# One-core attention and two weight stages on Trainium2: when the first weights are decoded, and which engine adds up the value means

## The chip, the cores and the metric

The kernel runs on one core of one Trainium2 chip. A core has TensorE (matmuls, PE in the profile; its weight loads are PEld), VectorE (DVE), ScalarE (ACT), GpSimd (POOL), and SyncE (SP), which issues the DMAs. The engines run side by side, each works through its own queue in order, and they wait for each other with semaphores. The metric is the device time of one execution in microseconds (us). Three runs of the kernel before gave 589.56, 590.07 and 591.69 us; the median is 590.07.

## The reference

The inputs are q, k, v of shape (2, 8, 768, 64) and seven weight matrices in 64-bit floats. What is computed, cut to the core:

```
k_sum = k.reshape(B, H, 24, 32, D).max(axis=3)        # block maxima of the keys
v_sum = v.reshape(B, H, 24, 32, D).mean(axis=3)       # block means of the values
scores = concat([scale*q@k.T where |i-j| < 16 else -1e9, scale*q@k_sum.T + log(32)])
x = softmax(scores) @ concat([v, v_sum])              # -> 1536 tokens x 512
h = max(x @ w1, x @ w2, x @ w3) @ w_out               # 512 -> 768 -> 512
y = ((h @ w_a) * (h @ w_b)) @ w_out2                  # 512 -> 1536 -> 512
```

## The kernel before

Each of the two sequences (batch entries) is cut into two chunks of 384 tokens, and each chunk's attention into four groups, one per pair of heads. So the first sequence has groups 0 to 7: groups 0 to 3 are the first chunk, 4 to 7 the second. `steps(b)` traces the attention of a sequence in small steps; one group passes through `scores` (TensorE products, a masked minimum on VectorE in L190, the exponential on ScalarE in L191), `normal` (a reciprocal on VectorE in L199, the scaling on GpSimd in L201), `transposes` (TensorE L211, copies to `aT` by VectorE L213 and ScalarE L215) and `values` (TensorE L228, then the split of x into a high and a low part by ScalarE L368 and VectorE L369). The groups overlap by one stage. Keys, value windows and mean inputs are loaded only at a sequence's first chunk.

`means` gives the block means of the values: the transposed values arrive in the tile `full` by one DMA (L138), blocks are halved by GpSimd additions as often as `VSUM` says (L143: none for groups 0 and 1, five halvings for group 2, one for group 3), VectorE reduces the rest (L145), GpSimd copies the sums to a second place (L146), TensorE transposes them (L148), and ScalarE writes them, scaled by 1/32, among the value rows (L150).

A weight tile (128x512 64-bit numbers, tile `w`) takes three steps. `w_load` is the DMA (L286). `w_round` makes 32-bit numbers out of the halves: ScalarE L300 or VectorE L298 for the high half, ScalarE L302 for the low one, VectorE L304 and L305, and GpSimd L306 for the sum. `w_split` makes two parts that TensorE multiplies fast: ScalarE L310, and the remainder by GpSimd, or for every third weight by VectorE (L311). `weights(n)` traces n weights further, with the loads four ahead.

The first layer (`layers12`) has 18 units per chunk of tokens, then the second layer's four outputs. One unit uses one weight tile: 12 TensorE products of 128x384 (`ph`, L365), evacuated by ScalarE (L390) or by a maximum on VectorE (L392); every third unit ends in a split (L368, and L369 on GpSimd). Units of the first chunk run alone for six turns (`TURNS`), then in turn with those of the second chunk, so that a weight is then used twice.

What sets the order: the instructions are traced in program order with waits worked out by the language, and a scheduler then decides each engine's order before the kernel runs; only SP keeps the traced order. `tc.issue_after(ins)` forbids the scheduler to put what is traced in its block ahead of `ins` on the engine of `ins`. In the kernel before, `weights(1)` is traced at the attention's steps 12, 16, ..., 40 of the first sequence (`PRE`), with no such bound; the dense layers and later weights are traced after these 44 steps, the weights behind the last reciprocal (L566 and L571).

Of the kernel before, what the change touches and what calls it, by code (L numbers as in the profile page):

```python
# [9 lines left out]
F32 = mybir.dt.float32  # L10
# [5 lines left out]
ALU = mybir.AluOpType  # L16
AX = mybir.AxisListType

B, H, S, D = 2, 8, 768, 64
P = 128  # L20
DM, FF1, FF2 = 512, 768, 1536
NTOK = B * S
BLOCK, WINDOW = 32, 16
NB = S // BLOCK
NT = S // P
NP = H // 2
HALF = 64
WIN = HALF + 2 * WINDOW
NC = WIN + NB
SEG = P + NB  # L30
# [8 lines left out]
Z_AT, KEY0 = (2 * WINDOW, WIN), (P - 2 * WINDOW, P + NB + 2 * WINDOW)  # L39
# [15 lines left out]
W64, W32, WBUFS, QB, SM, GB, BANKS = (6, 3), (4, 3), (24, 10), 3, 2, (12, 9), (2, 2, 1, 2, 2)  # L55


AHEAD, PRE, TURNS = (4, 1), (9, 4), (6, (24, 42), (42, 60))

EARLY, BIAS_DVE, SPLIT_DVE = 16, ((0, 1, 0), (0, 1, 0), (0, 0, 0)), ((0, 0, 1), (0, 0, 1), (1, 1, 1))
AT_DVE, VSUM = ((1, 0), (1, 1)), (0, 0, 5, 1, 0)


C_ID, C_ALL = 4 * NC, 4 * NC + P

MASK = {(t, a): (2 * a + (t == (NT - 1 if a else 0))) * NC for t in range(NT) for a in range(2)}

# [2 lines left out]
def attention_then_maxout_then_bilinear(ctx: ExitStack, tc: tile.TileContext, qt, kt, vt, vwin, wall, const, out):  # L72
    nc = tc.nc
# [3 lines left out]
    V, A, G, T = nc.vector, nc.scalar, nc.gpsimd, nc.tensor  # L77

    one = ctx.enter_context(tc.tile_pool(name="one", bufs=1))
# [13 lines left out]
    ps_c = ctx.enter_context(tc.tile_pool(name="ps_c", bufs=BANKS[4], space=PSUM))  # L93
    ps_m = ctx.enter_context(tc.tile_pool(name="ps_m", bufs=BANKS[3], space=PSUM))

    kept = one.tile([P, C_ALL + 2 * NC + NP * (NT + 1) * SEG], F32, name="kept")
    cols = iter(range(kept.shape[-1]))

    def take(n):

        at = [next(cols) for _ in range(n)][0]
        return kept[:, at:at + n]

    cst = take(C_ALL)
    ident = cst[:, C_ID:C_ID + P]
# [6 lines left out]

    v_t = [one.tile([NC, MAXT, 2, 2, D], F32, name=f"v{p}") for p in range(NP)]
    vpad = [take(NC) for _ in range(2)]


    groups = [(c, p) for c in range(NCH) for p in range(NP)]
# [5 lines left out]
    x_t, exps, a_t, last = {}, {}, {}, [None]  # L123

    def keys(b, p):

        kk = k_t[p].rearrange("p (t k) -> p t k", k=SEG)
        nc.sync.dma_start(out=kk[:, :, 0:P], in_=kt[b, p].rearrange("r (t k) -> r t k", k=P))

        k2 = sm_p.tile([P, NT + 1, 4, 2], F32, tag="k2", name="k2")  # L130
        V.tensor_reduce(k2, kk[:, :, 0:P].rearrange("p t (n k) -> p t n k", k=WINDOW), AX.X, ALU.max)
        k2 = k2.rearrange("p t n o -> p (t n o)")[:, 7:7 + 2 * NB].rearrange("p (o n z) -> p o n z", o=1, z=2)
        V.tensor_reduce(kk[:, :, P:SEG], k2.to_broadcast([P, NT + 1, NB, 2]), AX.X, ALU.max)  # L133

    def means(b, p):

        full = w64_p.tile([P, S], F32, tag="full", name="full", bufs=2)
        nc.sync.dma_start(out=full, in_=vt[b, p])  # L138
        full = full.rearrange("p (n k) -> p n k", k=BLOCK)
        k = BLOCK  # L140
        for _ in range(VSUM[p if b == 0 else NP]):
            k //= 2
            G.tensor_tensor(full[:, :, 0:k], full[:, :, 0:k], full[:, :, k:2 * k], ALU.add)  # L143
        z0, z1 = (vpad[p % 2][:, o:o + NB] for o in Z_AT)
        V.tensor_reduce(z0, full[:, :, 0:k], AX.X, ALU.add)  # L145
        G.tensor_copy(z1, z0)  # L146
        ps = ps_t.tile([NC, P], F32, tag="t", name="psvs")
        T.transpose(ps, vpad[p % 2], ident)  # L148
        for a, o in enumerate(Z_AT):
            A.activation(v_t[p][o:o + NB, :, a].rearrange("k i h d -> k i (h d)"),  # L150
                         ps[o:o + NB].rearrange("k (o e) -> k o e", o=1).to_broadcast([NB, MAXT, P]),
                         AF.Copy, scale=1.0 / BLOCK)

    def load(g):

        c, p = groups[g]
        b, t, n = CHUNKS[c]
        if t == 0:
            keys(b, p)
        nc.sync.dma_start(out=q_t[g % QB][:, 0:n], in_=qt[b, p].rearrange("r (t a m) -> r t a m", t=NT, a=2)[:, t:t + n])  # L160
        if g == 0:
            nc.sync.dma_start(out=cst, in_=const)

    def load_values(g):
        c, p = groups[g]
        b, t, n = CHUNKS[c]
        vw = vwin[b, p].rearrange("r (i a h d) -> r i a h d", a=2, h=2, d=D)[:, t:t + n]
        for a, z in enumerate(Z_AT):
            for r0, r1, to in ((0, z, 0), (z, WIN, z + NB)):
                if r0 < r1:  # L170
                    nc.sync.dma_start(out=v_t[p][to:to + r1 - r0, 0:n, a], in_=vw[r0:r1, :, a])
        if t == 0:
            means(b, p)

    def scores(g, i):

        c, p = groups[g]
        t, q = CHUNKS[c][1] + i, q_t[g % QB]
        if i == 0:
            exps[g] = (sm_p.tile([P, MAXT, 2, NC], F32, tag="s", name="s"),  # L180
                       sm_p.tile([P, MAXT, 2], F32, tag="sm", name="sm"))
        s, sm = (x[:, i] for x in exps[g])
        ps = ps_s.tile([P, 2, NC], F32, tag="s", name="ps")
        nm = sm_p.tile([P, 2], F32, tag="nm", name="nm", bufs=4)
        for a in range(2):
            k0 = t * SEG + KEY0[a]
            T.matmul(ps[:, a], q[:, i, a], k_t[p][:, k0:k0 + NC], start=True, stop=True)  # L187
            mask = cst[:, MASK[t, a]:MASK[t, a] + NC]

            V.tensor_tensor_reduce(s[:, a], ps[:, a], mask, -1.0 / D ** 0.5, 3e38, ALU.add, ALU.min, nm[:, a:a + 1])  # L190
            A.activation(s[:, a], s[:, a], AF.Exp, bias=nm[:, a:a + 1], scale=-1.0, accum_out=sm[:, a:a + 1])  # L191

    def normal(g):

        n = CHUNKS[groups[g][0]][2]
        s, sm = (x[:, 0:n] for x in exps[g])
        r = sm_p.tile([P, MAXT, 2, 1], F32, tag="r", name="r")[:, 0:n]
        A.activation(r, sm.rearrange("p i (a o) -> p i a o", o=1), AF.Copy, bias=1e-9)
        last[0] = V.reciprocal(r, r).ins  # L199
        s, r = s.rearrange("p i a k -> p (i a) k"), r.rearrange("p i a o -> p (i a) o")  # L200
        G.tensor_tensor(s, s, r.to_broadcast([P, 2 * n, NC]), ALU.mult)  # L201

    def transposes(g):
        at, n = exps.pop(g)[0], CHUNKS[groups[g][0]][2]
        a_t[g] = aT = sm_p.tile([NC, MAXT, 2, P], F32, tag="aT", name="aT")
        for i0 in range(0, n, 2):
            i1 = min(n, i0 + 2)
            ps = ps_t.tile([NC, 2, 2, P], F32, tag="t", name="pst")
            for i in range(i0, i1):
                for a in range(2):  # L210
                    T.transpose(ps[:, i - i0, a], at[:, i, a], ident)  # L211
            if AT_DVE[g >= len(groups) // 2][i0 // 2 % 2]:
                V.tensor_copy(aT[:, i0:i1], ps[:, 0:i1 - i0])  # L213
            else:
                A.activation(aT[:, i0:i1], ps[:, 0:i1 - i0], AF.Copy)  # L215
# [17 lines left out]
    def steps(b):  # L233


        first, end = (c * NP * len(SIZES) for c in (b, b + 1))
        load(first)
        if b == 0:
            load(first + 1)
        load_values(first)  # L240
        yield
        for g in range(first - 1, end):
            if g >= first:
                transposes(g)
                if b == 0 and g + 2 < first + NP:
                    load(g + 2)
                if (b or g + 1 >= first + NP) and g + 1 < end:
                    load(g + 1)
                if g + 1 < end:
                    load_values(g + 1)  # L250
                yield
            for i in range(MAXT):
                if g + 1 < end and i < CHUNKS[groups[g + 1][0]][2]:
                    scores(g + 1, i)
                    if i == CHUNKS[groups[g + 1][0]][2] - 1:
                        normal(g + 1)
                yield
            if g >= first:
                values(g)
                yield  # L260
# [74 lines left out]
    def weights(most):  # L335

        nonlocal w_done, w_room
        for _ in range(most):
            if w_done == len(seq) or w_room + room[w_done] > w_freed + WBUFS[w_done >= N12] or w_done == N12 and not gate:
                return  # L340
            w_room += room[w_done]
            w_done += 1
            ahead = min(AHEAD[0], W64[w_done + AHEAD[0] > N12] - 2)
            for n, (step, more) in enumerate(((w_load, ahead), (w_round, AHEAD[1]), (w_split, 0))):
                while w_at[n] < min(w_done + more, len(seq) if gate else N12):
                    step(w_at[n])
                    w_at[n] += 1
# [208 lines left out]
            q += 2  # L556


    for i in range(2):
        V.memset(vpad[i], 0.0)  # L560
    for n, _ in enumerate(steps(0)):
        weights(1 if n >= PRE[0] and n % PRE[1] == 0 else 0)


    turns = TURNS[0] * "0" + (N1 - TURNS[0]) * "01" + TURNS[0] * "1" + "00001111" + (N1 + 4) * "2" + (N1 + 4) * "3"
    behind = last[0]  # L566
# [73 lines left out]
```

## Time and profile before

| what | value |
|---|---|
| median of 3 runs | 590.07 us (589.56 to 591.69) |
| profiled execution | 591.21 us |
| its span in the trace | 589.3 us |
| PE busy | 551.3 us (94%) |
| DVE busy | 377.8 us (64%) |
| ACT busy | 278.7 us (47%) |
| POOL busy | 208.2 us (35%) |
| share of TensorE in the chain that ended last | 63% |

Busy time of TensorE is a union of pipelined matmuls, so 94% says that it seldom stood empty, not that it ran at its peak. The shares are averages over the whole span: the first 60 us, where attention starts up, and the 500 us after them look very different, so the stretches have to be read one by one.

### The profile page before, as it was taken

The page shows a single profiled execution, that of the slowest core. Times are in us where ns is not written, and L with a number is a line of the kernel's source. Part 1 is how long each engine was busy: PE and PEld are TensorE (multiplying, and loading weights), DVE is VectorE, ACT ScalarE, POOL GpSimd, SP SyncE. Part 2 cuts the span into 40 slices and gives each one's busy share as a digit, 9 for nine tenths or more (in the row PEclk, how much of TensorE's full clock was granted, in tenths as well). Part 3 has the DMA queues.
Part 4 walks back from the last instruction along what each step waited for, and adds up shares of the span by engine and source line. Part 5 has one row for each costly group of instructions (what it writes and reads, how often), then busy time and mean ns, then how long its engine had stood idle before and what let it go on. Part 6 is the DMA issues. An engine that isn't in the chain of part 4 may idle for free.

```text
span 589.3 us, 8831 instructions
## 1 busy us (share of the span) xinstructions
PE 551.3 (94%) x3272; PEld 513.3 (87%) x3272; DVE 377.8 (64%) x780; ACT 278.7 (47%) x667; POOL 208.2 (35%) x184
## 2 busy tenths in 40 slices
PE   4778999999999999998889899999999999999997
PEld 3567989999999999997888789999999989999985
DVE  4786398857213331249998775777696796883374
ACT  3777657444434332246675565653543544331220
POOL 0497269943001221035652433332341351330030
PEclk9959999999999999999999999999999999999999
DMA  9998035933211000052121123122212212000005
GB/s 265 344 273 247 36 110 190 298 73 107 63 47 48 1 1 1 1 222 85 52 72 43 66 72 108 37 72 72 71 41 77 98 37 72 2 1 0 1 17 198
DMA packets 31291, 53.32 MB, mean 90 GB/s; under 512 B 2448, under 2 KB 18832, under 8 KB 31248
## 3 DMA queue, kind: packets, MB, share of 16 engines
q1 hardware_dynamic: 31248, 52.75, 28.2%
q8 instruction: 26, 0.43, 0.3%
q14 instruction: 17, 0.14, 0.1%
HBM read 49.59 MB, written 3.15 MB: 89 GB/s over the span
## 4 chain that ended last, share of the span: by engine, by line
PE 63%; DVE 14%; DMA 7%; issue 5%; POOL 5%; ACT 5%; SPq 1%; POOLq 0%; ACTq 0%; DVEq 0%
PE ph L365 15%; PE qb L365 13%; PE py L365 7%; PE qg L365 5%; PE po L529 5%; DMA w<-wall 5%; PE po L527 5%; PE po L528 5%; POOL w L306 3%; DVE wt L311 3%; PE qd L365 3%; PE ps L187 2%; PE psv L228 2%; DVE hg L369 2%; DVE w L305 2%
## 5 line engine op out<-in xcount | busy, mean ns | idle before, releaser
L365 PE MATMUL ph<-x,wt 128*128 128x384 f32 x864 | 164.2, 343 | 3.8 <-DVE nm L190 2.0
L365 PEld LDWEIGHTS ph<-x,wt 128*128 128x128 f32 x864 | 150.7, 191 | 5.3 <-ACT wt L310 2.2
L306 POOL TENSOR_TENSOR w<-w,w 128x512 int32<-128x512 int32 x60 | 86.7, 1450 | 122.6 <-DVE w L305 73.5
L365 PE MATMUL qb<-yt,wt 128*128 128x384 f32 x576 | 114.2, 339 | 7.3 <-DVE t L496 2.0
L365 PEld LDWEIGHTS qb<-yt,wt 128*128 128x128 f32 x576 | 101.6, 188 | 14.0 <-DVE t L496 3.2
L368 ACT ACTIVATE hg<-t 128x384 fp32r<-128x384 f32 x72 | 36.9, 521 | 81.0 <-DVE t L392 36.0
L499 POOL TENSOR_TENSOR t<-t,ca 128x384 f32<-128x384 f32 x36 | 42.8, 1204 | 88.4 <-DVE t L498 85.7
L365 PE MATMUL qg<-yt,wt 128*128 128x384 f32 x288 | 59.4, 339 | 1.4 <-DVE t L498 0.6
L539 DVE TENSOR_TENSOR acc<-po,acc 128x512 f32<-128x512 f32 x60 | 40.8, 687 | 26.9 <-PE po L529 26.7
L527 PE MATMUL po<-wt,hg 128*128 128x512 f32 x144 | 56.4, 392 | 0.5 <-ACT hg L368 0.5
L528 PE MATMUL po<-wt,hg 128*128 128x512 f32 x144 | 56.5, 393 | 0.0
L529 PE MATMUL po<-wt,hg 128*128 128x512 f32 x144 | 55.8, 395 | 0.2 <-DVE hg L369 0.2
L365 PE MATMUL py<-hg,wt 128*128 128x384 f32 x288 | 55.1, 341 | 0.3 <-ACT hg L368 0.3
L365 PEld LDWEIGHTS qg<-yt,wt 128*128 128x128 f32 x288 | 50.9, 189 | 4.1 <-DVE t L498 0.9
L191 ACT ACTIVATE s<-s,nm 128x120 f32<-128x120 f32 x96 | 37.1, 388 | 33.3 <-DVE nm L190 32.9
L365 PEld LDWEIGHTS py<-hg,wt 128*128 128x128 f32 x288 | 49.6, 188 | 0.8 <-ACT hg L368 0.6
L392 DVE TENSOR_TENSOR t<-ph,t 128x384 f32<-128x384 f32 x48 | 26.3, 552 | 36.0 <-PE ph L365 31.6
L369 POOL TENSOR_TENSOR hg<-t,hg 128x384 fp32r<-128x384 f32 x24 | 26.8, 1116 | 61.8 <-ACT hg L368 61.8
L187 PE MATMUL ps<-kept,q 128*128 128x120 f32 x192 | 38.3, 319 | 10.6 <-DVE kept L133 7.7
L311 DVE TENSOR_TENSOR wt<-w,wt 128x512 fp32r<-128x512 f32 (+1 forms) x44 | 35.2, 799 | 20.0 <-ACT wt L310 20.0
L190 DVE CUSTOM_DVE_ANT_0 s<-ps,kept 128x120 f32<-128x120 f32 x96 | 24.6, 278 | 36.0 <-PE ps L187 35.4
L310 ACT ACTIVATE wt<-w 128x512 fp32r<-128x512 f32 (+1 forms) x60 | 35.0, 583 | 25.0 <-POOL w L306 12.6
(72 smaller groups left out, 789.1 us busy)
## 6 DMA issues: line engine op xcount, KB each, us to landing
w<-wall SPq DMA_DIRECT2D x60, 512.0 KB, 3.4
q<-qt SPq DMA_DIRECT2D x16, 384.0 KB, 7.2
kept<-kt SPq DMA_DIRECT2D x8, 448.0 KB, 6.9
full<-vt SPq DMA_DIRECT2D x8, 384.0 KB, 6.2
out<-acc SPq DMA_DIRECT2D x12, 256.0 KB, 2.0
v<-vwin SPq DMA_DIRECT2D x16, 144.0 KB, 5.4
v<-vwin SPq DMA_DIRECT2D x16, 96.0 KB, 5.7
v<-vwin SPq DMA_DIRECT2D x16, 48.0 KB, 6.7
```

What stands on the lines that cost most here:

```text
L187: T.matmul(ps[:, a], q[:, i, a], k_t[p][:, k0:k0 + NC], start=True, stop=True)
L191: A.activation(s[:, a], s[:, a], AF.Exp, bias=nm[:, a:a + 1], scale=-1.0, accum_out=sm[:, a:a + 1])
L306: G.tensor_tensor(w.bitcast(I32), w.bitcast(I32), lw.bitcast(I32), ALU.add)
L311: eng.tensor_tensor(w[:, 1], r, w[:, 0], ALU.subtract)
L365: T.matmul(ps, w[:, i, o:o + P], x[:, j], start=first and n == 0, stop=last and n == 2, skip_group_check=more)
L368: A.activation(dst[:, 0], src, AF.Copy)
L369: eng.tensor_tensor(dst[:, 1], src, dst[:, 0], ALU.subtract)
L499: G.tensor_tensor(t, t, cs[c, f], ALU.mult)
L527: T.matmul(ps, g[:, 0], w[:, 0], start=(f == 0), stop=False)
L528: T.matmul(ps, g[:, 0], w[:, 1], start=False, stop=False)
L529: T.matmul(ps, g[:, 1], w[:, 0], start=False, stop=(f == 1))
L539: V.tensor_tensor(acc[c, i], ps, acc[c, i], ALU.add)
```

## The change

Four things are edited.

- `PRE` is (18, 5): `weights(1)` is traced at steps 18, 23, 28, 33, 38 and 43 of the first sequence's attention, six times instead of eight. Step 17 holds the last reciprocal of the first chunk.
- Each of these calls stands in `tc.issue_after(behind)`, where `behind` is the last reciprocal traced in the step before.
- For the first sequence, `full` is loaded in another layout (tokens on partitions) from `vwin`, in two DMAs of 64 rows, and TensorE adds up the blocks: six products with a slice of a 0/1 matrix `ones` take the place of the VectorE reduction, the GpSimd additions and copy, and the transposition. `VSUM` is gone.
- `ones` is made once, of the identity matrix, by a memset, a reduction and a copy on VectorE. The second sequence's means are as they were with no GpSimd halving, which is what `VSUM[4] = 0` said before.

```diff
-AHEAD, PRE, TURNS = (4, 1), (9, 4), (6, (24, 42), (42, 60))
+AHEAD, PRE, TURNS = (4, 1), (18, 5), (6, (24, 42), (42, 60))
-AT_DVE, VSUM = ((1, 0), (1, 1)), (0, 0, 5, 1, 0)
+AT_DVE = ((1, 0), (1, 1))
...
         full = w64_p.tile([P, S], F32, tag="full", name="full", bufs=2)
-        nc.sync.dma_start(out=full, in_=vt[b, p])
-        full = full.rearrange("p (n k) -> p n k", k=BLOCK)
-        k = BLOCK
-        for _ in range(VSUM[p if b == 0 else NP]):
-            k //= 2
-            G.tensor_tensor(full[:, :, 0:k], full[:, :, 0:k], full[:, :, k:2 * k], ALU.add)
-        z0, z1 = (vpad[p % 2][:, o:o + NB] for o in Z_AT)
-        V.tensor_reduce(z0, full[:, :, 0:k], AX.X, ALU.add)
-        G.tensor_copy(z1, z0)
+        if b == 0:
+
+            vw = vwin[b, p, WINDOW:WINDOW + HALF].rearrange("r (i a e) -> r i a e", a=2, e=P)
+            for a in range(2):
+                nc.sync.dma_start(out=full[a * HALF:(a + 1) * HALF].rearrange("r (i e) -> r i e", e=P), in_=vw[:, :, a])
+        else:
+            nc.sync.dma_start(out=full, in_=vt[b, p])
         ps = ps_t.tile([NC, P], F32, tag="t", name="psvs")
-        T.transpose(ps, vpad[p % 2], ident)
+        if b == 0:
+
+            for t in range(NT):
+                at = NB - NS - t * NS
+                T.matmul(ps, ones[:, at:at + NC], full[:, t * P:(t + 1) * P], start=t == 0, stop=t == NT - 1)
+        else:
+            z0, z1 = (vpad[p % 2][:, o:o + NB] for o in Z_AT)
+            V.tensor_reduce(z0, full.rearrange("p (n k) -> p n k", k=BLOCK), AX.X, ALU.add)
+            G.tensor_copy(z1, z0)
+            T.transpose(ps, vpad[p % 2], ident)
...
             load(first + 1)
+            z0, z1 = (ones[:, NB - NS + z:NB + z] for z in Z_AT)
+            V.tensor_reduce(z0, ident.rearrange("p (j k) -> p j k", k=BLOCK), AX.X, ALU.add)
+            V.tensor_copy(z1, z0)
...
     for n, _ in enumerate(steps(0)):
-        weights(1 if n >= PRE[0] and n % PRE[1] == 0 else 0)
+        if n >= PRE[0] and (n - PRE[0]) % PRE[1] == 0:
+
+            with tc.issue_after(behind):
+                weights(1)
+        else:
+            behind = last[0]
```

On VectorE, the stretch from the key maxima of group 3 to the reciprocals of groups 2 and 3 stands so before (L190 is a score's masked minimum, L298, L304, L305 and L311 are weights, L369 is the split of x):

```order
L133 TENSOR_REDUCE kept<-k_252 128x7x24
L213 COPY aT<-pst 120x512
L369 TENSOR_TENSOR x<-psv,x 128x384
...
L304 TENSOR_SCALAR w_315<-psw 128x512
L145 TENSOR_REDUCE kept<-full 128x24
L305 SCALAR_TENSOR_TENSOR w_315<-psw,w_315 128x512
L298 TENSOR_SCALAR psw<-w_304 128x512
...
L199 RECIPROCAL r<-r 128x6
L305 SCALAR_TENSOR_TENSOR w_516<-psw,w_516 128x512
L145 TENSOR_REDUCE kept<-full 128x24
L311 TENSOR_TENSOR wt<-w_390,wt 128x512
L304 TENSOR_SCALAR w_574<-psw 128x512
L199 RECIPROCAL r<-r 128x6
```

and so in the changed kernel (its L199 is the minimum, L208 the reciprocal, L222 the copy to aT, L381 the split of x, L316, L310 and L317 weights):

```order
L135 TENSOR_REDUCE kept<-k_263 128x7x24
...
L208 RECIPROCAL r<-r 128x6
L381 TENSOR_TENSOR x<-psv,x 128x384
L199 ISA s,nm<-ps,kept 128x120
...
L222 COPY aT<-pst 120x512
L208 RECIPROCAL r<-r 128x6
L316 TENSOR_SCALAR w_411<-psw 128x512
L310 TENSOR_SCALAR psw<-w_400 128x512
L317 SCALAR_TENSOR_TENSOR w_411<-psw,w_411 128x512
```

No weight instruction stands ahead of the fourth reciprocal any more; before, fourteen did.

On TensorE, the end of the first sequence's attention stands so before (psv are a group's value products, ph the first layer):

```order
L211 MATMUL pst<-kept,s 120x128 x6
L365 MATMUL ph<-x,wt 128x384 x12
L228 MATMUL psv<-aT,v_112 64x64 x12
L365 MATMUL ph<-x,wt 128x384 x210
```

and so in the changed kernel:

```order
L220 MATMUL pst<-kept,s 120x128 x6
L377 MATMUL ph<-x,wt 128x384 x11
L237 MATMUL psv<-aT,v_112 64x64 x12
L377 MATMUL ph<-x,wt 128x384 x264
```

Ahead of the last of these psv rows stand 114 ph products before and 60 in the changed kernel, so the uninterrupted row behind it is 54 longer. The last 2451 rows of TensorE's 3006 are the same in both.

## Rows read from the trace of the kernel before

**Rows 1.** The page: TensorE's granted clock and DMA busy share, 40 slices.
```profile
PEclk9959999999999999999999999999999999999999
DMA  9998035933211000052121123122212212000005
```
**Rows 2.** Stretches: start:end us, length, busy us (and count) per engine, granted clock, DMA share, GB/s.
```profile
core 0: us, PE busy (x) PEld busy (x) DVE busy (x) ACT busy (x) POOL busy (x), PEclk, DMA share, GB/s
0.00:28.00 28.00, 16.17 (x107) 13.46 (x107) 16.96 (x59) 15.15 (x49) 7.33 (x15) 1.00 0.98 306
28.00:46.00 18.00, 13.04 (x66) 10.71 (x66) 14.34 (x40) 14.82 (x44) 16.01 (x14) 0.53 0.90 257
...
60.00:83.00 23.00, 21.53 (x191) 19.78 (x187) 13.48 (x39) 12.75 (x43) 7.31 (x6) 1.00 0.17 56
83.00:589.30 506.30, 489.67 (x2818) 460.36 (x2818) 324.88 (x612) 225.75 (x500) 168.70 (x144) 1.00 0.21 69
0.00:60.00 60.00, 40.09 (x268) 33.20 (x268) 39.47 (x130) 40.21 (x126) 32.21 (x35) 0.86 0.93 283
...
83.00:120.00 37.00, 37.00 (x215) 36.90 (x216) 31.72 (x50) 23.46 (x44) 35.78 (x29) 1.00 0.77 221
```
**Rows 3.** The chain of waits in time: start us, us, engine, tile and line.
```profile
37.24 1.81 POOL s L201
...
81.39 0.94 PE psv L228 x24
...
82.89 15.94 PE ph L365 x90
```
**Rows 4.** VectorE's timeline: start us, us, line, operation, idle before and its releaser.
```profile
19.10 1.09 DVE L131 TENSOR_REDUCE k<-kept 128x56 f32<-128x896 f32 x1
...
38.31 0.18 DVE L199 RECIPROCAL r<-r 128x6 f32<-128x6 f32 x1
...
51.46 0.56 DVE L369 TENSOR_TENSOR x<-psv,x 128x384 fp32r<-128x384 f32 x1 [0.16 <-ACT x L368]
```
**Rows 5.** Groups of VectorE, 24.5 to 38.4 us: count, busy us, mean ns, idle before.
```profile
L304 DVE TENSOR_SCALAR w<-psw 128x512 uint32<-128x512 uint32 x6 | 4.0, 685 | 1.6 <-ACT psw L300 1.6
L305 DVE SCALAR_TENSOR_TENSOR w<-psw,w 128x512 uint32<-128x512 uint32 x5 | 3.4, 676 | 0.0
...
L311 DVE TENSOR_TENSOR wt<-w,wt 128x512 fp32r<-128x512 f32 x1 | 1.9, 1855 | 0.2 <-ACT wt L310 0.2
L298 DVE TENSOR_SCALAR psw<-w 128x512 f32<-128x512 f32 x2 | 1.4, 690 | 0.0
```
**Rows 6.** Groups of VectorE, 0 to 83 us.
```profile
L190 DVE CUSTOM_DVE_ANT_0 s<-ps,kept 128x120 f32<-128x120 f32 x48 | 12.2, 278 | 8.9 <-PE ps L187 8.7
...
L213 DVE COPY aT<-pst 120x512 f32<-120x512 f32 x8 | 5.5, 682 | 6.1 <-PE pst L211 6.1
L131 DVE TENSOR_REDUCE k<-kept 128x56 f32<-128x896 f32 x4 | 4.3, 1086 | 4.7 <-DMA kept<-kt 4.7
...
L369 DVE TENSOR_TENSOR x<-psv,x 128x384 fp32r<-128x384 f32 x7 | 3.9, 553 | 1.8 <-ACT x L368 1.8
...
L145 DVE TENSOR_REDUCE kept<-full 128x24 f32<-128x768 f32 x2 | 1.9, 954 | 0.8 <-DMA full<-vt 0.8
```
**Rows 7.** Groups of GpSimd, 0 to 83 us.
```profile
L306 POOL TENSOR_TENSOR w<-w,w 128x512 int32<-128x512 int32 x10 | 13.3, 1333 | 6.9 <-ACT s L191 2.4 <-DVE w L305 2.3 <-ACT aT L215 1.9
...
L311 POOL TENSOR_TENSOR wt<-w,wt 128x512 fp32r<-128x512 f32 x7 | 9.0, 1285 | 0.7 <-ACT wt L310 0.7
L143 POOL TENSOR_TENSOR full<-full 128x384 f32<-128x384 f32 x2 | 2.0, 1017 | 2.4 <-DMA full<-vt 2.4
```
**Rows 8.** Groups of TensorE: 0 to 83 us, 28 to 46, 83 to 120.
```profile
L187 PE MATMUL ps<-kept,q 128*128 128x120 f32 x96 | 21.9, 361 | 10.6 <-DVE kept L133 7.7 <-DVE nm L190 2.2 <-DMA q<-qt 0.7
...
L365 PE MATMUL ph<-x,wt 128*128 128x384 f32 x13 | 5.3, 551 | 2.8 <-DVE nm L190 2.0 <-POOL wt L311 0.8
...
L365 PE MATMUL ph<-x,wt 128*128 128x384 f32 x211 | 37.1, 335 | 0.6 <-ACT x L368 0.6
```
**Rows 9.** SyncE's timeline.
```profile
17.31 3.97 SPq L286 DMA_DIRECT2D w<-wall x5
```

More of the change, by code (lines that the diff above doesn't have):

```diff
@@ L55 @@
 W64, W32, WBUFS, QB, SM, GB, BANKS = (6, 3), (4, 3), (24, 10), 3, 2, (12, 9), (2, 2, 1, 2, 2)
-AHEAD, PRE, TURNS = (4, 1), (9, 4), (6, (24, 42), (42, 60))
+AHEAD, PRE, TURNS = (4, 1), (18, 5), (6, (24, 42), (42, 60))
 EARLY, BIAS_DVE, SPLIT_DVE = 16, ((0, 1, 0), (0, 1, 0), (0, 0, 0)), ((0, 0, 1), (0, 0, 1), (1, 1, 1))
-AT_DVE, VSUM = ((1, 0), (1, 1)), (0, 0, 5, 1, 0)
+AT_DVE = ((1, 0), (1, 1))
 C_ID, C_ALL = 4 * NC, 4 * NC + P
+NS = P // BLOCK
 MASK = {(t, a): (2 * a + (t == (NT - 1 if a else 0))) * NC for t in range(NT) for a in range(2)}
@@ L94, in attention_then_maxout_then_bilinear @@
     ps_m = ctx.enter_context(tc.tile_pool(name="ps_m", bufs=BANKS[3], space=PSUM))
-    kept = one.tile([P, C_ALL + 2 * NC + NP * (NT + 1) * SEG], F32, name="kept")
+    kept = one.tile([P, C_ALL + 2 * NC + NC + NB - NS + NP * (NT + 1) * SEG], F32, name="kept")
     cols = iter(range(kept.shape[-1]))
@@ L114, in attention_then_maxout_then_bilinear @@
     vpad = [take(NC) for _ in range(2)]
+    ones = take(NC + NB - NS)
     groups = [(c, p) for c in range(NCH) for p in range(NP)]
@@ L556, in layers34 @@
             q += 2
-    for i in range(2):
-        V.memset(vpad[i], 0.0)
+    for x in (*vpad, ones):
+        V.memset(x, 0.0)
     for n, _ in enumerate(steps(0)):
-        weights(1 if n >= PRE[0] and n % PRE[1] == 0 else 0)
+        if n >= PRE[0] and (n - PRE[0]) % PRE[1] == 0:
[3 more added lines that the diff above has]
+            behind = last[0]
     turns = TURNS[0] * "0" + (N1 - TURNS[0]) * "01" + TURNS[0] * "1" + "00001111" + (N1 + 4) * "2" + (N1 + 4) * "3"
```

## The prediction

> **What bounds the kernel now.** I read the stretches first, then the chain of waits, then VectorE's timeline, then the groups that give durations. From 60 us on TensorE is the bound: it is busy 21.53 of 23 us and then 489.67 of 506.3 [rows 2]. In the first 60 us it is not: 40.09 busy us, so 19.9 stand empty, and in 28 to 46 us what it does runs at a mean granted clock of 0.53, almost all of it at the lower of the two levels, 1.2 GHz; there a ph product costs 5.3/13 = 0.41 us of busy time, while in 83 to 120 us it costs 37.1/211 = 0.176 [rows 2, 8]. What the change can win lies in that start, about 20 us of idle time and some us of half clock, and nowhere else; the later order on TensorE is the same in both kernels.
>
> The start ends, for my purpose, when the value products of group 7 are done and the uninterrupted row of ph begins: 82.9 us [rows 3]. I call this time T. After it TensorE is full, so the end moves with T and with the products that T leaves over. That makes the whole sum: shift = (T after - 82.9) + (products moved behind T) x 0.176.
>
> Why is T so late? The keys of group 3 are there at 19.1 us, when VectorE begins to reduce them, but the reciprocal of group 3 comes at 38.31 and its x is split at 51.46 [rows 4]. Between 24.5 and 38.4 VectorE runs 14 weight instructions, 4.0 + 3.4 + 1.9 + 1.4 = 10.7 us [rows 5]. The chain then passes a GpSimd scaling that took 1.81 us in a queue full of weights [rows 3]; GpSimd is 89% busy there, 16.01 of 18 us [rows 2]. So the first chunk's attention waits behind weights that nobody can use before x exists. DMA is the rival suspect: it is busy 93% of the first 60 us and nearly all of the first 28 [rows 1, 2].
>
> **The change part by part.**
>
> *Weights behind the reciprocals.* After the reduction of group 3's keys at 19.1 VectorE has, up to the reciprocal of group 3, that reduction (1.09), 14 masked minima (14 x 0.278 = 3.9), two copies to aT (1.4) and two splits of x (1.1) [rows 4, 6]: 7.5 us, 26.6, and with a short second key reduction 27. Later loads (below) and waits for ScalarE make it 28 in my sum; the bounds are 27 and the 38.3 of before. From there to the last copy to aT of group 7 the changed order puts on VectorE: 7 + 7 + 3 weight operations of 0.685, 0.676 and 0.690, one weight remainder of 1.855, together 13.5; 24 minima, 6.7; five copies to aT, 3.4; five splits of x, 2.8; two maxima of the first layer, taken at the price of a split, 1.1 [rows 5, 6]. That is 27.5 us. VectorE was filled to 14.34/18 = 80% in 28 to 46 us and to 31.72/37 = 86% in 83 to 120 [rows 2]; at 83% the 27.5 take 33.1, so the last copy ends at 61.1, and with group 7's 0.94 of value products [rows 3] T after = 62. Bounds: VectorE without a gap, 27 + 27.5 + 0.9 = 55.4; and at 80% from a reciprocal that is as late as before, 38.3 + 34.4 + 0.9 = 73.6. I take 62, since the two measured fillings lie close together.
>
> *Fewer units ahead of T.* 114 ph stood ahead of T, now 60. The 54 others follow it at 0.176: +9.5 us [rows 8]. Six weights are asked for ahead of T instead of eight, and unit 5 needs the sixth. GpSimd spends 1.333 + 2/3 x 1.285 = 2.19 us on a weight [rows 7], VectorE (2 x 0.68 + 0.69/3 + 1.855/3) = 2.2. A unit takes TensorE 12 x 0.176 = 2.1, so as long as the first chunk's units run alone the supply only just keeps up; from unit 6 on each weight serves two units, 4.2 us, and the supply runs away from the demand even with the splits that GpSimd also does. I put this at nothing, hidden behind TensorE; if the lead at T is missing it costs up to three units, 6 us.
>
> *TensorE adds the means.* Removed: on VectorE four reductions, the two large ones 0.954 each, on GpSimd six halvings of which the two large ones take 1.0 each [rows 6, 7], and four copies; on TensorE four transpositions. Added: 24 f32 products of 128 columns. The nearest row is L187, also f32 with 120 columns: the 48 products of the program are 96 records, 21.9/96 = 0.228 us of busy time each [rows 8], so 48 records cost 10.9 us. They all lie ahead of the first chunk's last values. TensorE was busy 16.17 of the first 28 us [rows 2], so 11.8 were free. Bounds: 0 if they fall into these gaps, 10.9 if all of them delay the fourth group. Each batch stands ahead of products of the next group and waits for its `full` tile, but only the last two batches can sit on the path of group 3, and there the next copies and minima run beside them. I take 1 us, the one that is in the 28 above. Below nothing isn't excluded: the GpSimd halvings stood between the scalings of groups 1 and 2, but GpSimd's path for group 3 is cleared by the first edit already.
>
> *Loads.* Each of four groups has one DMA more, and group 3's values now go ahead of the first weight load, which was issued at 17.31 [rows 9]. Those are eight issues; five weight loads took SyncE 3.97 us [rows 9], 0.8 each, so the first weight is issued about 6 us later, at 24, and lands at about 31, near the reciprocal at 28 that it has to wait for anyway. The bytes are the same. It can cost up to 3 us on the first weight, and it is inside the 80% of the upper bound.
>
> *The rest* (a third memset, making `ones` once: three small VectorE instructions while the first loads are under way) I put at nothing, 0.5 us if the first minimum waits for it.
>
> **Sum.** 62 - 82.9 + 9.5 = -11.4 us. The profiled execution took 591.21 us, of which 589.3 are the span and 1.9 lie around it; it becomes 579.8. It lies 1.14 above the median of 590.07, so against the median the forecast is 578.7. Break-even is T = 82.9 - 9.5 = 73.4.
>
> **A rule against the change.** TensorE's clock was at the lower level in 28 to 46 us, after a stretch in which the engine had stood empty for 11.8 of 28 us [rows 2]. The change takes ph products out of just this time. The Trainium skill (TensorE: Matmul & The Clock Gate, "Why this matters for your kernels") advises against idle gaps between bursts of matmuls, because the engine then falls back to half rate; the trace agrees, 0.53 in 28 to 46 us. By that rule the thinner work would stay slow up to T, which is the second rival below; by the rows TensorE has nearly the same attention work in less time, and the 48 new records besides, so I expect fewer gaps than before.
>
> **The rivals.**
>
> *The weights become the wait.* T comes at 62 but units 0 to 5 run late, because each of the first weights now stands behind one more reciprocal and group 7 is done when only five units are. For it: VectorE's 2.2 us and GpSimd's 2.19 per weight are no less than the unit's 2.1. Against it: from unit 6 on the demand halves. Price up to 6 us: 584.7.
>
> *Half clock up to T.* The 60 ph cost 0.41 instead of 0.176, 14.0 us more, if the level stays low from the first chunk's end to T. For it: the granted clock in rows 1 and 2. Against it: the low stretch began where TensorE had idle gaps behind weights. Half of the 14.0 would be covered by waits for VectorE: T = 69, shift -4.4, 585.7; all of it on the path: T = 76.0, +2.6, 592.7. I take the midpoint, 589.
>
> *Slower: the loads held the first chunk, not VectorE.* Then x of group 3 is split at 51.5 as before, and the second chunk with its units follows. In my sum it takes from group 3's reciprocal to T 34 us, and from that reciprocal to its x some 8, so 26 from x to T: T = 77.5, +4.1, 594.2. It decides from an x of group 3 later than 47.4. For it: DMA at 0.98 of the first 28 us [rows 2], and group 3's values one place further in the queue. Against it: group 3's keys are there at 19.1, and the later rows of the chain are GpSimd and TensorE, not DMA [rows 3, 4].
>
> *It doesn't do what it says*: the weights that are now later shift the same queue time behind T, and nothing is left of the gain, 590. Against it: the 19.9 idle us of TensorE can't come back once it is full.
>
> **How the numbers follow.** Forecast 578.7, chance 0.66, own range 572 (T = 55.4) to 584. Weights 0.12; half clock 0.10; loads 0.06; nothing 0.06. What this kernel's measurement can tell from no change is about 0.5%, 3 us: faster means below 587.1, slower above 593.0. Faster: 0.66 + 0.12 + half of the half clock = 0.83. Same: the other half of it but a little, and the case of nothing, 0.10. Slower: loads and the worst clock, 0.07. The range goes from the lower bound on T, 572, to 588, which takes in the weights and part of the half clock and leaves out 0.15 to 0.2.
>
> **What would show it.** In the new profile: no weight instruction on VectorE ahead of the fourth reciprocal, and that reciprocal at 27 to 31 us; x of group 3 split at 35 to 40; the value products of group 7 ending at 56 to 67; from there TensorE without gaps and 264 ph in a row of 46 to 47 us; the first 60 us with 8 to 12 idle us of TensorE instead of 19.9; the second half of the span unchanged. It is wrong if the reciprocal stays near 38, if TensorE waits for weights (L318, L323) behind T, or if the granted clock stays low beyond 46 us.

## The result and the profile after

The changed kernel takes 596.42 us (median of 10 runs, 593.15 to 599.18), the kernel before 591.61 us beside it (10 runs, 589.56 to 594.76). The ratio is 1.0084, with a 95% interval of 1.006 to 1.0108: it is slower by 4.8 us. The forecast of 578.7 us was wrong in its sign as well as in its size. The profiled execution took 594.63 us, its span 592.8, which is 3.5 more than before.

The page of the changed kernel, TensorE's granted clock and the DMA engines' busy share in 40 slices, against [rows 1]:

```profile
PEclk9879899999999999999999999999999999999999
DMA  9996255923211000043221222122212212000005
```

Its stretches, with the columns of [rows 2]:

```profile
0.00:28.00 28.00, 16.60 (x102) 14.97 (x103) 13.53 (x56) 12.07 (x44) 2.98 (x6) 0.95 1.06 249
28.00:46.00 18.00, 13.56 (x128) 11.62 (x127) 8.24 (x31) 13.58 (x40) 7.02 (x6) 0.80 0.96 312
60.00:83.00 23.00, 20.95 (x175) 19.33 (x175) 19.28 (x46) 17.14 (x44) 18.25 (x15) 0.94 0.47 154
0.00:60.00 60.00, 41.45 (x313) 36.99 (x314) 30.71 (x122) 35.73 (x123) 15.30 (x16) 0.91 0.91 251
```

Read the first two rows against [rows 2]. VectorE's work in 28 to 46 us fell from 14.34 to 8.24 us and GpSimd's from 16.01 to 7.02: both were relieved as foreseen, and the granted clock of that stretch rose from 0.53 to 0.80. Yet TensorE's idle time in the first 60 us fell only from 19.9 to 18.55. The last two numbers of the first row say where to look: in the first 28 us the DMA engines are as full as before (1.06 against 0.98), and they move 249 GB/s where they moved 306.

TensorE's timeline (start us, us, line, operation, idle before and its releaser) before and at the point called T, and the next wait behind it, against [rows 3]:

```profile
58.14 3.08 PE L377 MATMUL ph<-x,wt 128*128 128x384 f32 x11 [2.12 <-DVE wt L323]
...
74.70 0.92 PE L237 MATMUL psv<-aT,v 120*64 120x64 f32 x24
75.55 46.34 PE L377 MATMUL ph<-x,wt 128*128 128x384 f32 x264
122.91 0.70 PE L196 MATMUL ps<-kept,q 128*128 128x120 f32 x4 [1.02 <-DVE kept L135]
```

T is 75.55. The prediction's own formula gives (75.55 - 82.9) + 54 x 0.176 = +2.2 us, and the wait of 1.02 us at 122.91, which the kernel before doesn't have, makes +3.2 of the span's +3.5. The accounting holds; T was wrong by 13.6 us. Ahead of T, at 58.14, TensorE waited 2.12 us for a weight whose remainder VectorE made (L323).

VectorE's timeline, against [rows 4]:

```profile
20.26 1.09 DVE L133 TENSOR_REDUCE k<-kept 128x56 f32<-128x896 f32 x1 [1.36 <-DMA kept<-kt]
...
33.83 0.19 DVE L208 RECIPROCAL r<-r 128x6 f32<-128x6 f32 x1 [2.77 <-ACT r L207]
...
38.25 0.19 DVE L208 RECIPROCAL r<-r 128x6 f32<-128x6 f32 x1 [0.77 <-ACT r L207]
...
47.64 0.56 DVE L381 TENSOR_TENSOR x<-psv,x 128x384 fp32r<-128x384 f32 x1 [1.74 <-ACT x L380]
...
113.60 4.86 DVE L323 TENSOR_TENSOR wt<-w,wt 128x512 fp32r<-128x512 f32 x1 [1.45 <-ACT wt L322]
```

VectorE's groups between 24.5 and 38.3 us, against [rows 5]:

```profile
L199 DVE CUSTOM_DVE_ANT_0 s<-ps,kept 128x120 f32<-128x120 f32 x10 | 2.5, 278 | 3.5 <-PE ps L196 3.5
...
L208 DVE RECIPROCAL r<-r 128x6 f32<-128x6 f32 x2 | 0.4, 192 | 3.5 <-ACT r L207 3.5
```

The 10.7 us of weights have left VectorE, and the reciprocal of group 3 comes at 38.25, against 38.31 before. The time turned into waiting: 3.5 us for scores and 3.5 us for ScalarE's `r`. Most of the wait for scores is one of 2.84 us ahead of 30.55; up to 30.03 TensorE ran a group's means (2.08 us) and value products (0.92 us) ahead of these scores. ScalarE's timeline says what that engine does instead of `r`:

```profile
29.06 0.65 ACT L312 ACTIVATE psw<-w 128x512 f32<-128x512 f32 x1 [1.67 <-DMA w<-wall]
...
31.92 0.65 ACT L314 ACTIVATE w<-w 128x512 int32<-128x512 uint32 x1 [0.87 <-DMA w<-wall]
33.59 0.21 ACT L207 ACTIVATE r<-sm 128x6 f32<-128x6 f32 x1
...
40.58 0.69 ACT L314 ACTIVATE w<-w 128x512 int32<-128x512 uint32 x1 [2.36 <-DMA w<-wall]
```

`tc.issue_after(behind)` holds back VectorE's weight instructions alone. ScalarE's share of a weight stands in its queue ahead of the sums' `r`, and waits there for a weight load. The loads come later than before, as SyncE's timeline shows against [rows 9]; the two issues of group 3's means take 1.21 us ahead of them. Most of the delay is not theirs: in e1 below, with the old means, the five loads are issued at 21.85, since the weights stand later in the program.

```profile
21.98 1.21 SPq L144 DMA_DIRECT2D full<-vwin  x2
23.23 2.62 SPq L298 DMA_DIRECT2D w<-wall  x5
```

The new products of the means, in TensorE's groups from 0 to 83 us, are 48 records of 9.4 us, a little under the 10.9 worked out from [rows 8]:

```profile
L152 PE MATMUL psvs<-full,kept 128*120 128x128 f32 x48 | 9.4, 371 | 2.1 <-DMA full<-vwin 1.6 <-DVE aT L222 0.4
```

### The profile page after: what moved, and what is told of

The parts are those of the page before. It is cut to its first block, busy times and chain, and to the rows that moved or that the text cites. A ratio compares the mean times of both kernels' runs of the same rounds, so it can differ in the third digit from the quotient of the medians.

```text
span 592.8 us, 8919 instructions
## 1 busy us (share of the span) xinstructions
PE 554.5 (94%) x3316; PEld 518.6 (87%) x3316; DVE 378.5 (64%) x779; ACT 279.0 (47%) x667; POOL 203.4 (34%) x174
## 4 chain that ended last, share of the span: by engine, by line
PE 66%; DVE 12%; DMA 8%; ACT 5%; issue 5%; POOL 2%; SPq 1%; POOLq 0%; DVEq 0%; ACTq 0%
PE ph L377 19%; PE qb L377 12%; PE py L377 6%; DMA w<-wall 5%; PE qg L377 5%; PE po L541 5%; PE po L540 5%; PE po L539 5%; PE ps L196 3%; DVE wt L323 3%; PE qd L377 2%; PE psv L237 2%; DVE hg L381 2%; POOL w L318 2%; DVE t L510 1%
## 5 line engine op out<-in xcount | busy, mean ns | idle before, releaser
L377 PE MATMUL ph<-x,wt 128*128 128x384 f32 x864 | 161.2, 341 | 2.9 <-DVE wt L323 2.1
L210 POOL TENSOR_TENSOR s<-s,r 128x720 f32<-128x720 f32 x16 | 22.2, 1390 | 91.5 <-DVE r L208 87.2
L323 DVE TENSOR_TENSOR wt<-w,wt 128x512 fp32r<-128x512 f32 (+1 forms) x44 | 37.8, 859 | 22.4 <-ACT wt L322 22.3
L196 PE MATMUL ps<-kept,q 128*128 128x120 f32 x192 | 36.0, 304 | 12.6 <-DVE kept L135 8.2
L199 DVE CUSTOM_DVE_ANT_0 s<-ps,kept 128x120 f32<-128x120 f32 x96 | 24.5, 278 | 36.2 <-PE ps L196 35.3
L381 POOL TENSOR_TENSOR hg<-t,hg 128x384 fp32r<-128x384 f32 x24 | 26.7, 1111 | 60.6 <-ACT hg L380 58.4
```

What stands on the lines that cost most here:

```text
L323: eng.tensor_tensor(w[:, 1], r, w[:, 0], ALU.subtract)
L377: T.matmul(ps, w[:, i, o:o + P], x[:, j], start=first and n == 0, stop=last and n == 2, skip_group_check=more)
L381: eng.tensor_tensor(dst[:, 1], src, dst[:, 0], ALU.subtract)
```

## The experiments

All were timed in five rounds against the kernel before, and ratios are to it. "g3" is group 3. The theory from the profile of the changed kernel: the first chunk's attention is held by loads (the means' two transfers per group and the late weight loads), partly through ScalarE's queue. Its rivals: the 24 products on TensorE's path, or the bound on VectorE itself. A number from a trace is that of one execution, which can lie 2 to 3 us beside its kernel's median (588.36 against 590.75 in e6, 591.85 against 594.79 in e12).

| kernel | median us | ratio (95% interval) |
|---|---|---|
| the change | 596.42 | 1.0084 (1.006 to 1.0108) |
| e1, weights' part alone | 589.70 | 0.9969 (0.995 to 0.9987) |
| e2, means' part alone | 600.94 | 1.0149 (1.0111 to 1.0187) |
| e3, change, ScalarE bound too | 592.04 | 1.0018 (1.0002 to 1.0034) |
| e4, change without the bound | 594.90 | 1.0067 (1.004 to 1.0094) |
| e5, e2 with one load, 3 KB pieces | 595.17 | 1.0072 (1.0049 to 1.0094) |
| e6, change with that load | 590.75 | 1.0005 (0.9975 to 1.0036) |
| e7, e1, ScalarE bound too | 586.07 | 0.9929 (0.9902 to 0.9957) |
| e8, e7, weights loaded one ahead | 584.05 | 0.9885 (0.9856 to 0.9915) |
| e11, e6 in 512 B pieces | 591.91 | 1.0022 (1.0005 to 1.0039) |
| e12, e6 in two halves of the rows | 594.79 | 1.0053 (1.0024 to 1.0082) |
| e13, e5 with half of the products | 594.06 | 1.0057 (1.0038 to 1.0076) |
| e14, e8 with e6's means | 583.18 | 0.9872 (0.9853 to 0.9891) |

**e1 and e2, each part alone.** e1 keeps the later, bound weights and has the old means; e2 the reverse.

```
e1:  AT_DVE, VSUM = ((1, 0), (1, 1)), (0, 0, 5, 1, 0)     # and the old means()
e2:  AHEAD, PRE, TURNS = (4, 1), (9, 4), ...              # and weights(1) with no bound
```

> The change without its means: weights traced at steps 18, 23, ... behind the reciprocals, the block means by VectorE and GpSimd as before. Theory A (ScalarE's weight conversions wait for their loads ahead of the first chunk's sums): they stand there still, so the reciprocal of group 3 comes at 33 to 36 us, T (start of the long row of ph) at 71 to 74, time 589 to 593. Theory B (the 24 new TensorE products hold the scores): without them the reciprocal comes at 28 to 31, T at 65 to 69, time 582 to 587. Theory C (the later and more numerous loads): as A, T near 73.

> The means by TensorE alone, weights traced as in the kernel before, no bound. A: the new products are hidden beside the weights, same as before within 0.3%. B: T later than 82.9 by 3 to 6 us, time 594 to 598. C: one DMA more per group, 0 to 2 us slower.

The two parts have opposite signs: the weights' part gains 0.31%, the means' part alone costs 1.49%. e1 came out as A and C have it, which its numbers can't separate (g3's reciprocal at 35.67, T at 73.63); B is out. e2 took longer than any of its three theories gave. In e2 T is 93.32 with 114 ph ahead as before: 93.32 - 82.9 = +10.4 us, and its span is 10.9 longer.

**e3 and e4, the bound.** e3 also queues weights behind ScalarE's `r`; e4 takes the bound away and leaves the weights' later place in the program.

```
e3:  with tc.issue_after(behind), tc.issue_after(behind_act):
         weights(1)
e4:  weights(1)
```

> The change, with the weights bound on ScalarE too, behind the sum's copy of the same group. A: reciprocal of group 2 at 27 us instead of 33.8, of group 3 at 29 to 33 instead of 38.3, T at 66 to 71 with the same or a few more ph ahead of it, time 585 to 592. B and C: the reciprocal of group 3 stays at 36 to 38, T at 74 to 77, time 594 to 598.

> The change without the bound: PRE is (18, 5), means by TensorE, VectorE's weights free to stand ahead of the reciprocals. 93 ph instead of 60 ahead of the long row. If the bound on VectorE is what costs (the weights then late), time near 591, as before; if it gains, slower than the change, above 597; A: VectorE's order decides little, as ScalarE holds the sums in both, so the sum T + 0.176 x products left stays within 1.5 us of the change's, 594 to 597.

e4 and the change can't be told apart in time (1.0067 and 1.0084), as the expectation had it, but not for its reason: VectorE's order did decide when g3's reciprocal came. VectorE's timeline of e4, where weights stand ahead of it again, has it 9 us later than the change (38.25):

```profile
47.33 0.19 DVE L208 RECIPROCAL r<-r 128x6 f32<-128x6 f32 x1
```

T is 82.21 instead of 75.55, so the bound brought T forward by 6.7 us. It also left 33 more ph behind T (60 instead of 93 ahead), 33 x 0.176 = 5.8 us, and the two nearly cancel. No run takes the bound away with the old means.

Queueing the weights behind ScalarE's `r` too took 0.66% off; the time lies at the upper edge of A, T (75.66) where B and C had it. g2's reciprocal then came at 30.34 instead of 33.83, but g3's at 39.95. Its sum was ready on ScalarE at 37.05; on VectorE minima of the next group stood ahead of the reciprocal, and their scores waited for `q`, as TensorE's timeline of e3 shows:

```profile
38.56 0.68 PE L196 MATMUL ps<-kept,q 128*128 128x120 f32 x4 [2.37 <-DMA q<-qt]
```

**e5 and e6, the means' load.** A group's values come token by token from an array laid out for it on the host, in one transfer over 128 rows in pieces of 3 KB; bytes and products are the same.

```
-  for a in range(2):
-      nc.sync.dma_start(out=full[a * HALF:(a + 1) * HALF]..., in_=vw[:, :, a])
+  nc.sync.dma_start(out=full, in_=vtok[p])
```

> As e2_means_only, but the mean inputs lie in memory as TensorE wants them and arrive in one DMA of 128 rows with 3 KB pieces, instead of two of 64 rows with 512 B pieces. Theory L (these loads lower the DMA rate while everything waits for loads): the rate of the first 30 us is 285 to 305 GB/s instead of 248, the keys of group 3 are there by 19.5 us instead of 22, and the time is 591 to 595. Theory P (the 24 products hold TensorE): the rate may rise, the time stays at 598 to 602.

> The change with the mean inputs in one DMA of 128 rows with 3 KB pieces. L: 587 to 592, about as e1_weights_only. P: 594 to 598, as the change.

The load is worth about half of the means' cost taken alone (1.0149 to 1.0072), and in the change nearly all of its loss: 1.0084 to 1.0005. e6 came out as L; e5 lies between L and P, just above L's range. With the same bytes to move, e6 has 294 GB/s in its first 28 us instead of 249 (row below), g3's reciprocal at 34.29 and T at 70.38.

**e7 and e8, the weights' part carried further.** e7 is e1 with the ScalarE bound of e3. e8 also lets weight loads run one ahead instead of four during the first sequence's attention.

```
e8:  if n == 0 and few[0]:
         more = few[0]      # 1 until steps(0) is over, then ahead (4)
```

> As e1_weights_only (means as before), with the weights bound on ScalarE too. Theory S (ScalarE's weight conversions hold the sums): reciprocals of groups 2 and 3 at 27 to 29 and 29 to 32 us, T at 66 to 69, time 583 to 588. Theory Q (q of group 4 lies behind five weight loads): reciprocals earlier as well, but TensorE then waits for q to about 36 us, T at 71 to 74, time 588 to 592.

> As e7_old_means_scalar_too, with weight loads one ahead instead of four until the attention of the first sequence is traced, so two weight loads stand before q of group 4 instead of five. Q: q of group 4 lands 4 to 6 us earlier, T at 65 to 70, time 582 to 588. If the weights are the wait instead: TensorE waits for L312 behind T or in the first units, time 588 to 593.

e7 came out as S, with reciprocals at 28.67 and 32.13 and T at 67.60. Its TensorE then waits for `q` of groups 4 and 5:

```profile
34.54 0.68 PE L188 MATMUL ps<-kept,q 128*128 128x120 f32 x4 [0.38 <-DMA q<-qt]
...
38.93 0.45 PE L188 MATMUL ps<-kept,q 128*128 128x120 f32 x2 [0.86 <-DMA q<-qt]
```

SyncE's timeline of e7 shows five weight loads ahead of the `q` of group 4. In e8 (second fence) there are two, and then one ahead of each `q`:

```profile
20.35 3.02 SPq L287 DMA_DIRECT2D w<-wall  x5
23.47 0.38 SPq L161 DMA_DIRECT2D q<-qt  x1
```

```profile
20.79 0.91 SPq L287 DMA_DIRECT2D w<-wall  x2
21.74 0.43 SPq L161 DMA_DIRECT2D q<-qt  x1
```

In e8 the waits for `q` are gone, g4's reciprocal comes at 39.88 instead of 43.65, and the median is 2.0 us lower; the intervals of e7 and e8 overlap, so of that step the trace is the better evidence. T is 68.47 with 72 ph ahead: -14.4 + 42 x 0.176 = -7.0, and the median is 6.8 us below the one before (0.0115 x 591).

**e11 and e12, pieces or halves.** The change differs from e6 in two ways, so each was put back alone.

```
e11: in_=vtok[p].rearrange("(t r) e -> r t e", r=P)       # pieces of 512 B, 128 rows
e12: for a in range(2):                                   # pieces of 3 KB, 64 rows
         nc.sync.dma_start(out=full[a * HALF:(a + 1) * HALF], in_=vtok[p, a * HALF:(a + 1) * HALF])
```

> The change, with the means' input of a group in one transfer over all 128 rows, but in pieces of 512 B (1.0005 with one transfer in 3 KB pieces, 1.0084 as changed, with two transfers over 64 rows in 512 B pieces). Theory, the short pieces cost: 1.006 to 1.010, and some 250 to 265 GB/s over the first 30 us. Rival, the split over two halves of the rows costs: 0.998 to 1.003, and near 300 GB/s.

> The change, with the means' input of a group in two transfers over 64 rows each, in pieces of 3 KB. Theory, the short pieces cost and the halves don't: 0.998 to 1.003, near 300 GB/s over the first 30 us. Rival, the halves cost: 1.006 to 1.010, some 250 to 265 GB/s.

The theory that the short pieces cost and the halves don't was the wrong way round. The runs of e12 average 2.4 us above those of e11 (interval 0.7 to 4.0), taken beside the same runs of the kernel before. e12's 1.0053 is less than its rival gave, and its interval still touches that of e6; e11's 1.0022 can't be told from e6. The stretch from 0 to 28 us of e6, e11 and e12, in this order, with the columns of [rows 2]:

```profile
0.00:28.00 28.00, 17.78 (x141) 15.65 (x141) 14.13 (x60) 14.03 (x51) 2.98 (x6) 1.00 0.99 294
```

```profile
0.00:28.00 28.00, 16.38 (x126) 14.52 (x127) 13.50 (x56) 12.07 (x44) 2.98 (x6) 1.00 1.04 265
```

```profile
0.00:28.00 28.00, 16.22 (x102) 14.70 (x103) 13.54 (x56) 12.07 (x44) 2.98 (x6) 0.95 1.01 248
```

The busy share is full in all three; 294 GB/s become 265 with short pieces and 248 with halves. A part of this is what is in flight: the first weight loads are issued at 20.49 us in e6, 22.09 in e11 and 23.69 in e12, and e1, with the old means in one transfer, moved 276 where the kernel before moved 306. In the first 20 us, with no weight load issued in any of the three, the difference is about half as large and has the same order (e6, e11, e12):

```profile
0.00:20.00 20.00, 11.79 (x79) 10.40 (x79) 10.27 (x39) 7.35 (x26) 1.59 (x5) 1.00 0.97 274
```

```profile
0.00:20.00 20.00, 10.85 (x54) 9.58 (x54) 8.76 (x33) 7.17 (x25) 1.59 (x5) 1.00 0.99 258
```

```profile
0.00:20.00 20.00, 10.39 (x49) 9.43 (x50) 8.76 (x33) 7.17 (x25) 1.59 (x5) 1.00 0.98 253
```

Over all runs, VectorE begins to reduce g3's keys at 18.25 to 19.82 us in the eight with one transfer in long pieces, at 20.03 in e11, and at 20.26 to 22.52 in the five with halves. SyncE also spends about 1.1 to 1.2 us on issuing two halves. In e6 the one issue of g3 took 0.35:

```profile
20.10 0.35 SPq L142 DMA_DIRECT2D full<-vtok  x1
```

The Trainium skill (DMA: Bandwidth & Descriptors, "Rules for kernel authors") says that two transfers to disjoint halves of the partitions run one after the other and that one over 128 partitions should be used. The trace agrees that one is better, 274 against 253 GB/s in the first 20 us; whether the halves ran one after the other it doesn't show, as each landed 5.0 to 6.8 us after its issue and the two of a group were issued about 0.5 us apart. The Trainium skill (DMA: Bandwidth & Descriptors, "Specifications") puts the smallest transfer for the full rate at 512 B; here pieces of exactly that size moved 258 against 274 GB/s in the first 20 us of the one profile of each, and their times don't settle it.

**e13, half of the products.** It leaves out half of the tokens of the first sequence's means.

```
-  for t in range(NT):
+  for t in range(0, NT, 2):
```

> TensorE's means alone with one transfer in 3 KB pieces (1.0072 with 24 products), but 12 products in place of 24: it leaves out half of the tokens of the first sequence's means. Theory, what is left of the cost is the products' time ahead of the next group's scores: some 4 x 1.4 us less at the cold clock, of which a part is on the path, so 1.001 to 1.004. Rival, it is the order and the wait for the means' input, whatever the number of products: 1.006 to 1.009.

1.0057 against 1.0072 of e5, with intervals that overlap and between the two ranges given: the products' time is not shown to be the rest of the means' cost. TensorE's timeline of e13 ahead of T, and its stretches, show another thing, beside the row of 210 in the kernel before (first fence):

```profile
82.89 36.73 PE L365 MATMUL ph<-x,wt 128*128 128x384 f32 x210 [0.59 <-ACT x L368]
```

```profile
80.29 0.92 PE L235 MATMUL psv<-aT,v 120*64 120x64 f32 x24 [2.07 <-DVE aT L220]
82.10 39.65 PE L375 MATMUL ph<-x,wt 128*128 128x384 f32 x210 [0.89 <-ACT x L378]
```

```profile
75.00:83.00 8.00, 4.01 (x39) 3.31 (x40) 7.85 (x13) 3.41 (x9) 4.75 (x4) 0.89 0.01 2
83.00:90.00 7.00, 6.88 (x27) 6.37 (x26) 6.97 (x12) 5.32 (x10) 7.00 (x6) 0.64 0.17 56
```

T is 0.8 us earlier than before, with the same 114 ph ahead, but TensorE was busy only 4.01 of 8 us while the full VectorE (7.85 of 8) finished group 7, and then the clock fell: 0.64 in 83 to 90 us. The row of 210 ph took 39.65 us, against 36.73 before. So -0.8 + 2.9 = +2.1 of a span that is 1.8 longer. In e5 T is 2.9 later and the row, at a clock of 0.76 in those 7 us, takes 38.27, +1.5; together +4.4 of a span of +4.3. In e13, under the old weight order, TensorE's earlier start is spent waiting for VectorE, at whose end T still stands.

**e14, the means in the best version.**

> The version with few weight loads (0.9885: weights queued behind both engines, weight loads one ahead, the old means), with the means added up by TensorE from one transfer in 3 KB pieces. Theory, GpSimd's and VectorE's means were off the path and the products are on it: 0.990 to 0.995, slower than 0.9885. Rival, the work taken from VectorE and GpSimd now counts, since nothing else is late: 0.982 to 0.987.

0.9872 against 0.9885, intervals overlapping, and a hair above the rival's range: with one load of 128 rows, and nothing else late, the means on TensorE neither cost nor gain what can be measured. The formula for T fits it, from this row of TensorE's timeline:

```profile
67.51 43.95 PE L377 MATMUL ph<-x,wt 128*128 128x384 f32 x252
```

(67.51 - 82.9) + 42 x 0.176 = -8.0, and its span is 580.8, 8.5 less. Both e8 and e14 beat the two kernels of this case.

## Why the prediction was wrong

*What bounds the kernel.* Right: the end moved with T and the products behind it. The formula gave the span within 0.5 us in the change, e1, e2, e3, e6, e8, e11, e12 and e14, with the one wait that the change and e11 have behind T (1.0 and 1.3 us) counted in. It was off by 0.6 us in e7 and by 1.2 in e4, with their waits for weights behind T (0.9 and 1.0 us) counted in, and it missed in e5 and e13, where the clock fell at T.

*Weights behind the reciprocals.* This is the step that failed. It put g3's reciprocal at 28 because it counted VectorE's work, with only 1 us on top for later loads and waits for ScalarE; it came at 38.25, the sign of being wrong that the prediction named ("stays near 38"), and 10.3 of the 13.6 us by which T was wrong are that. From the reciprocal to T it took 37.3 us, against 34 in the sum: the other 3.3. Clearing VectorE mattered (without it, in e4, the reciprocal comes at 47.33), but it freed one of three things that stood late together. ScalarE's weights stayed ahead of the sums (e1 to e7, g3's reciprocal 35.67 to 32.13), and the loads held both (the change to e6, 38.25 to 34.29). No version came below 32.13, so the bound of 27 was not tested; what is last there wasn't taken apart.

*Loads.* "The bytes are the same" was true and beside the point: DMA was full, and I priced bytes instead of how a transfer is cut. Halves and short pieces cost 0.79% together (1.0005 to 1.0084), some 4.7 us, and "up to 3 us on the first weight" was the wrong place for it: the keys and `q` of every group came later too.

*TensorE adds the means.* 1 us was too little for the means as the change loads them: 1.15% between e1 and the change, 6.8 us. For the products the 0 to 10.9 was the right kind of bound, and e14 lies at its lower end.

*Fewer units ahead of T.* +9.5 held: 264 ph in a row of 46.34 us, as the prediction's list asked (46 to 47). The supply of weights was no wait at T, as foreseen; ahead of T it was one, the 2.12 us at 58.14, which the prediction had at nothing and which may be most of those 3.3. And at 113.60 VectorE's L323 took 4.86 us, and the second sequence's first key reduction had to stand behind it until 120.51: that is the wait of 1.02 us, one the prediction didn't have. In e6 and e12, whose TensorE has the same row of 264 ph, the subtraction at this place took 1.1 us and the wait is absent.

*The rivals.* "The loads held the first chunk" was nearest: it asked for an x of g3 later than 47.4, found at 47.64, and gave a shift of +4.1 us, against +4.8 of the medians and +3.5 of the span. That is partly luck: it had x at 51.5 and 26 us from there to T, and they were 47.64 and 27.9. It had 0.06. What spoke for it was in the rows (DMA at 0.98 of the first 28 us), and what I held against it, that keys were there at 19.1 and that the chain's last links were not DMA, was read in a trace where the weights covered the loads. "Half clock up to T" fell: 0.80 in 28 to 46 us and 0.94 in 60 to 83. "Weights the wait" fell as the main cause: 2.12 us instead of its 6, beside a T that was late already.

*The change's sign.* The idea wasn't bad, the change was half of it. Its weights' part, with ScalarE bound too and fewer loads ahead, is worth 1.15%; its means' part, loaded as here, ate more than the 0.31% that the first half brings.

## What to carry to other kernels

When an engine's queue is cleared ahead of a late result, look at every engine and load that feeds the same result, and expect the next one just behind: here VectorE, ScalarE and the loads were late within a few us of each other. Bring what moves behind the milestone into the sum as well: the bound on VectorE won 6.7 us of T and gave 5.8 back. Where the DMA engines are full, price a transfer by how it is cut over rows and pieces, not by its bytes. Split a change of two parts before judging it: these two had opposite signs.

## What the runs showed of the hardware

At a full DMA share (0.97 to 0.99), halves of the rows and short pieces lowered the rate of the first 20 us from 274 to 253 and 258 GB/s, in one profile of each. The busy share alone doesn't show it.

VectorE's subtraction of L323 took 4.86 us at 113.60 where another, at 103.61, took 1.11:

```profile
103.61 1.11 DVE L323 TENSOR_TENSOR wt<-w,wt 128x512 fp32r<-128x512 f32 x1
```

GpSimd's timeline beside both:

```profile
102.87 1.29 POOL L323 TENSOR_TENSOR wt<-w,wt 128x512 fp32r<-128x512 f32 x1
...
114.11 1.30 POOL L323 TENSOR_TENSOR wt<-w,wt 128x512 fp32r<-128x512 f32 x1
115.36 1.31 POOL L318 TENSOR_TENSOR w<-w,w 128x512 int32<-128x512 int32 x1
116.61 1.30 POOL L323 TENSOR_TENSOR wt<-w,wt 128x512 fp32r<-128x512 f32 x1
```

Three GpSimd instructions ran one after another within the long one, and it ended at 118.46, 0.55 us after the last of them. GpSimd was at work beside the short one too, and that one ended at 104.72, 0.56 us after the GpSimd instruction that was running when it began. Of the seven other L323 of VectorE from 56 to 124 us six ended so, 0.54 to 0.57 us behind one GpSimd instruction, and took 0.68 to 1.60 us; the one at 113.60 let three more go first. The Trainium skill (SBUF — State Buffer, "Who interferes with whom") says that a VectorE instruction with two SBUF inputs and a GpSimd instruction that reads SBUF block each other whole; the trace fits that, though no run here took GpSimd's work away to show it.

The granted clock fell to 0.64 of 83 to 90 us in e13 after 8 us in which TensorE was busy for 4.01, and to 0.76 in e5 after a busy 5.80 of 8; before, with 6.53 busy us of 8, it stayed at 1.00. Busy time alone doesn't sort these: in e4, with 5.20 busy us of the same 8, it stayed at 1.00 as well.
